# The end of a two-block decode attention: load order of the last pairs, V as the stationary operand in PV of five pairs, and wo as the stationary operand in the second block's output

## The chip, the cores and the metric

The kernel runs on one core of one Trainium2 chip. Its time is the device time of that core in microseconds (us), the median of several executions. A profile is one execution; the "span" that it shows is from the first to the last instruction and is about 1.8 us shorter than the time of the same execution. Times inside a profile count from the span's start. TensorE is PE (weight loads are PEld), VectorE is DVE, ScalarE is ACT, SyncE is SP.

## The reference, cut to what matters

Two independent attention blocks, A and B, each for one token, 32 heads, 8192 keys of 128 elements in bf16. The outputs stand side by side.

```
q      = x @ wq                                   # (512) @ (512 x 4096)
scores = einsum("bhqd,bhkd->bhqk", q, k_cache) * 128**-0.5
p      = softmax(scores)
o      = einsum("bhqk,bhkd->bhqd", p, v_cache)
y      = o.reshape(1, 1, 4096) @ wo               # (4096) @ (4096 x 512)
```

Each head's K is 2 MB and so is its V, and every byte is used once: 285 MB are read and almost nothing is written.

## The kernel before

Heads are handled in pairs: pairs 0 to 15 are block A, 16 to 31 block B. Below, "K30" is the 4 MB of keys of pair 30, "V30" its values. All loads go through a ring of five slots of 4 MB, in one fixed order on one queue; a slot is loaded anew when the last reader of its old content is done.

```
order = [('wq', a) for a in range(NA)]
for j in range(NPR + 1):                 # NPR = 32 pairs
    if j < NPR:      order.append(('k', j))
    if j == NPR - 1: order[-1:] = [('wo', LA), order[-1]]     # wo of B ahead of K31
    if j >= 1:       order.append(('v', j - 1))
    if j == PPA + 2: order.append(('wo', 0))
# so it ends: K30, V29, wo of B (first 24 heads), K31, rest of wo, V30, V31 in four parts
```

For one pair, VectorE multiplies K with q in place, in eight pieces (`plan_M`, about 1.17 us each); TensorE adds up the 128 products of each key with 2 x 16 matmuls against the identity (`plan_fold`; 3.6 us for one half at full clock); VectorE finishes the sums (`plan_R`), then come the maximum (`plan_m1`, a transpose `plan_tr`, `plan_m2`), exp on ScalarE, and PV on TensorE. PV has two forms. The wide one has p as the stationary operand, and its result must be copied out and turned:

```
def wide(e):                                   # pairs 0 to 29, plan_PV
    for i in range(0, TP, TB):                 # 32 matmuls, 512 columns each
        m = e.matmul(ot_ps[j % 2][0:2 * TB, :], p2[...i:i + TB...], t[:, i:i + TB, :]..., ...)
cp_val[j] = INC('ACT', c_cp, lambda e: e.copy(o8[:, j % 2, :], ot_ps[j % 2][0:2 * TB, :]))
...                                            # plan_ot: four f32 matmuls that turn o8

def op(e):                                     # pairs 30 and 31, plan_PVs
    for i in range(t0, t1):                    # up to 128 weight loads, 2 columns each
        m = e.matmul(ot_ps[j % 2][:, 0:2], t[:, i, :], p2[:, j % 2, i, :], ...)
```

y is o times wo. For all but the last four heads of B wo is loaded in a layout that makes its DMA pieces long, so o must be rearranged to fit it: `plan_w` does this for a block of n heads with n small matmuls on TensorE and some small operations on VectorE. y itself has a spread column of o as the stationary operand (4 columns wide, `sq`), with four matmuls of 128 columns for a head:

```
m = e.matmul(y_ps[0:NB, 0:P], sq[:, a, h0 + i, b * NB:(b + 1) * NB], wo[:, h0 + i, b, :], ...)
```

All engines work through fixed lists in order. TensorE's list ended: ..., PV29, max of pair 30 and 31 with y of B's heads 0 to 23 between, folds of K31, half of PV30, the block of heads 24 to 27, the rest of PV30, PV31 by parts, y of the last four heads.

## Time and profile before

| what | before | where it is read |
|---|---|---|
| time, median of the first 3 runs | 682.48 us (680.91 to 684.72) | timed runs |
| span | 680.3 us | page |
| DMA rate in midstream | about 431 GB/s | slice table |
| landing of V30; of V31's four parts | 659.3; 664.2, 666.6, 667.9, 669.1 | issue time plus time to landing |
| issue of the output's DMA | 678.42 us | timeline |

The lines below are from the page of before: the DMA's busy tenths, and the GB/s, in 40 equal slices.

```profile
span 680.3 us, 6183 instructions
...
DMA  9999999999999999999999999999999999999991
GB/s 370 432 432 431 432 431 432 433 430 432 431 432 429 432 434 433 432 431 432 431 430 431 432 433 431 432 431 432 431 429 433 432 432 431 432 431 420 421 423 63
```

The reader should see that there is no hole in the stream until the last slice. The Trainium skill, "DMA: Bandwidth & Descriptors", section "Where 436 GB/s comes from", gives 435 GB/s as the ceiling of the fabric; the 431 of this trace lie just below it, though above the 358 GB/s per core that the same section says binds loads from HBM, so here the measurement decides. The bytes can't shrink, so what can be saved is behind the stream.

The next view gives the same core in stretches of one microsecond (stretch, its length, busy time of PE, PEld, DVE, ACT, POOL with counts of instructions, granted clock, share of the DMA engines that were busy, GB/s).

```profile
662.00:663.00 1.00, 1.00 (x8) 0.39 (x3) 0.00 (x0) 0.49 (x3) 0.00 (x0) 1.00 0.98 406
...
664.00:665.00 1.00, 1.00 (x7) 0.00 (x0) 0.00 (x0) 0.00 (x0) 0.00 (x0) 1.00 0.63 258
...
667.00:668.00 1.00, 0.94 (x34) 0.84 (x31) 0.53 (x3) 0.00 (x0) 0.00 (x0) 1.00 0.19 78
668.00:669.00 1.00, 0.28 (x6) 0.31 (x6) 0.68 (x4) 0.00 (x0) 0.00 (x0) 1.00 0.10 41
```

The 16 engines do not finish together: the share falls from 0.98 to 0.10 within six microseconds. A load counts as landed when the last of its parts has: the packed trace marks 16 of them for each load. The 29.4 MB from K29's landing (599.5) to the last (669.1) came at 422 GB/s, and the prediction calls this the slowest engine's rate.

The third view is the chain of waits in order of time (start, length, what), here its tail.

```profile
615.75 31.09 DMA ring<-in_B_k_cache_dram
...
650.87 4.84 PE yps L615 x64
...
660.25 1.88 PE yps L615 x32
...
666.12 1.60 PE otps L514 x64
...
670.08 1.77 PE otps L514 x64
...
674.93 1.81 PE otps L514 x64
...
678.12 0.28 DVE y_sb L626
```

The last wait for data is K31's, which lands at 646.8. From there on everything is TensorE's and VectorE's own work: y of the first 24 heads (L615), PV30 and PV31 (L514). V31's first part, there at 664.2, is multiplied after 672. TensorE is late, not the data.

### The profile page before, as it was taken

Reading aid. Unit: us, or ns where it says so; the run is one execution under the profiler, and the core shown is the slowest. Engines: PE = TensorE matmul, PEld = TensorE weight load, DVE = VectorE, ACT = ScalarE, POOL = GpSimd, SP = SyncE. Lnnn points to the kernel's source line nnn. Section 1 sums busy time; section 2 is a strip of 40 time slices with the busy share of each in tenths; the row PEclk is TensorE's granted clock in tenths of the full one; section 3 lists DMA queues with packets and bytes.
Section 4 is the critical chain, followed back from the end, with each engine's and each line's share of the span. In section 5 each row is a group of like instructions: output and inputs, shape, how many; then the busy total and the mean of one; then the engine's idle time right before and its main releaser. Section 6 shows DMA issues by size and latency. Waiting matters only on the chain.

```text
span 680.3 us, 6183 instructions
## 1 busy us (share of the span) xinstructions
PE 561.4 (83%) x3020; PEld 168.8 (25%) x2060; DVE 386.4 (57%) x519; ACT 59.7 (9%) x199; POOL 2.4 (0%) x16
## 2 busy tenths in 40 slices
PE   0477998788799878887998496999789969876978
PEld 0120222122222212222221133232122212222246
DVE  4148656666555566665545626676655376663361
ACT  0020111101110111011101010111011101100000
POOL 1000000000000000000000000000000000000000
PEclk9998999889998988899988797999899979989887
DMA  9999999999999999999999999999999999999991
GB/s 370 432 432 431 432 431 432 433 430 432 431 432 429 432 434 433 432 431 432 431 430 431 432 433 431 432 431 432 431 429 433 432 432 431 432 431 420 421 423 63
DMA packets 11387, 285.61 MB, mean 420 GB/s; under 512 B 1504, under 2 KB 2016, under 8 KB 2400
## 3 DMA queue, kind: packets, MB, share of 16 engines
q1 hardware_dynamic: 11064, 285.22, 97.7%
q8 instruction: 20, 0.33, 0.2%
q10 hardware_dynamic: 296, 0.00, 0.0%
q14 instruction: 7, 0.06, 0.0%
HBM read 285.21 MB, written 0.00 MB: 419 GB/s over the span
## 4 chain that ended last, share of the span: by engine, by line
PE 44%; DMA 43%; DVE 11%; ACT 1%; issue 1%; ACTq 0%; DVEq 0%
DMA ring<-in_B_k_cache_dram 20%; DMA ring<-in_A_k_cache_dram 20%; PE fold L175 18%; PE otps L492 14%; DVE ring L387 8%; DMA xT<-in_B_x_dram 3%; PE qwps L359 3%; PE yps L615 2%; PE stps L532 2%; PE fold L171 2%; DVE s_sb L413 1%; PE otps L514 1%; DVE m L423 1%; ACT qbc L366 1%; PE stps L442 1%
## 5 line engine op out<-in xcount | busy, mean ns | idle before, releaser
L387 DVE TENSOR_TENSOR ring<-ring,qbc 128x2048 bf16<-128x2048 bf16 x256 | 298.3, 1215 | 154.1 <-DMA ring<-in_A_k_cache_dram 89.9
L175 PE MATMUL fold<-ring,ident 128*128 128x512 bf16 x960 | 245.9, 414 | 0.0
L492 PE MATMUL otps<-ring,p 128*8 128x512 bf16 x960 | 212.1, 379 | 0.0
L492 PEld LDWEIGHTS otps<-ring,p 128*8 128x8 bf16 x960 | 81.0, 87 | 116.4
L171 PE MATMUL fold<-ring,ident 128*128 128x512 bf16 x64 | 26.8, 419 | 53.3 <-DVE ring L387 53.3
L532 PEld LDWEIGHTS stps<-ident_f,o 8*128 8x128 f32 x240 | 28.9, 186 | 132.4 <-issue 132.4
L413 DVE TENSOR_REDUCE s_sb<-fold 128x64 f32<-128x512 f32 x64 | 44.0, 687 | 12.9 <-PE fold L175 12.5
L359 PE MATMUL qwps<-ring,xsel 128*128 128x512 bf16 x64 | 18.6, 442 | 29.1 <-DVE xsel L243 24.2
L502 ACT COPY o<-otps 8x512 f32<-8x512 f32 x30 | 17.3, 575 | 284.3 <-PE otps L492 284.3
L463 PEld LDWEIGHTS stps<-rowsum,ones_f 128*128 128x128 f32 x64 | 12.3, 194 | 98.7 <-issue 97.9
L432 PE MATMUL stps<-ident_f,m 128*2 128x128 f32 x32 | 9.2, 286 | 32.4 <-DVE m L423 32.3
L532 PE MATMUL stps<-ident_f,o 8*128 8x2 f32 x240 | 31.5, 249 | 0.0
L448 ACT COPY nb<-stps 128x1 f32<-128x1 f32 x32 | 5.1, 159 | 283.2 <-PE stps L442 283.2
L456 ACT ACTIVATE p<-s_sb,nb 64x128 bf16<-64x128 f32 x64 | 28.0, 437 | 1.9
L551 DVE TENSOR_TENSOR ot<-stps,rinv 128x2 bf16<-128x2 f32 x30 | 4.8, 159 | 40.3 <-PE stps L532 40.0
L171 PEld LDWEIGHTS fold<-ring,ident 128*128 128x128 bf16 x64 | 6.2, 97 | 62.3 <-DVE ring L387 58.2
L579 DVE TENSOR_TENSOR wt<-qwps,hmask 128x512 f32<-128x512 f32 (+3 forms) x5 | 2.2, 441 | 32.0 <-PE qwps L572 31.9
L423 DVE TENSOR_REDUCE m<-s_sb 64x1 f32<-64x128 f32 x64 | 17.9, 280 | 2.1
L615 PE MATMUL yps<-ring,sq 128*4 128x128 bf16 x256 | 17.3, 233 | 1.1 <-DVE sq L593 0.8
L615 PEld LDWEIGHTS yps<-ring,sq 128*4 128x4 bf16 x256 | 16.0, 91 | 1.8 <-issue 1.1
L359 PEld LDWEIGHTS qwps<-ring,xsel 128*128 128x128 bf16 x64 | 6.3, 108 | 40.8 <-issue 28.7
L432 PEld LDWEIGHTS stps<-ident_f,m 128*2 128x2 f32 x32 | 2.6, 80 | 48.6 <-DVE m L423 46.0
(37 smaller groups left out, 98.0 us busy)
## 6 DMA issues: line engine op xcount, KB each, us to landing
ring<-in_A_k_cache_dram SPq DMA_DIRECT2D x16, 4096.0 KB, 34.9
ring<-in_A_v_cache_dram SPq DMA_DIRECT2D x16, 4096.0 KB, 32.4
ring<-in_B_k_cache_dram SPq DMA_DIRECT2D x16, 4096.0 KB, 34.0
ring<-in_B_v_cache_dram SPq DMA_DIRECT2D x15, 4096.0 KB, 32.7
ring<-in_A_wq_dram SPq DMA_DIRECT2D x1, 4096.0 KB, 12.4
ring<-in_B_wq_dram SPq DMA_DIRECT2D x1, 4096.0 KB, 21.8
ring<-in_A_wo_dram SPq DMA_DIRECT2D x1, 4096.0 KB, 36.2
ring<-in_B_wo_dram SPq DMA_DIRECT2D x1, 2048.0 KB, 30.8
```

The costliest lines, as they stand in the source:

```text
L171: return e.matmul(out, lhsT, rhs, start=start, stop=stop)
L175: return e.add_instruction(mybir.InstMatmult(name=nc.get_next_instruction_name(), engine=e.engine, ins=[e.lower_ap(rhs), e.lower_ap(lhsT)] ...
L359: m = e.matmul(qw_ps[:, :].rearrange("p (j d) -> p j d", d=Dh), xsel[:, a, c, par, :], wq[:, c, 4 * g:4 * g + 4, par, :], start=(i == 0), ...
L387: m_val[(j, i)] = INC('DVE', c_m, lambda e: e.tensor_tensor(t, t, qbc[:, a, jj:jj + 1, :].broadcast_to([P, CH, Dh]), ALU.mult))
L413: r_val[(j, h)] = INC('DVE', c_r, lambda e: e.tensor_reduce(s_sb[:, j % 2, h * HT:(h + 1) * HT], fold_ps[h][:, :].rearrange("p (t e) -> p ...
L423: m1_val[j] = INC('DVE', c_m1, lambda e, h=h, q0=q0, q1=q1: e.tensor_reduce(m1[q0:q1, j % 2, h:h + 1], s_sb[q0:q1, j % 2, :], AX.X, ALU.max))
L456: e_val[j] = INC('ACT', c_e, lambda e, h=h, q0=q0, q1=q1: e.activation(p2[q0:q1, j % 2, :, h], s_sb[q0:q1, j % 2, :], AF.Exp, bias=nb[q0:q ...
L463: s_val[j] = INC('PE', c_s, lambda e: e.matmul(st_ps[j % 2][:, P + 2:P + 4], ones_f[:], rowsum[:, j % 2, :], start=True, stop=True))
L492: m = e.matmul(ot_ps[j % 2][0:2 * TB, :], p2[:, j % 2, i:i + TB, :].rearrange("p t h -> p (t h)"), t[:, i:i + TB, :].rearrange("p t d -> p ...
L502: cp_val[j] = INC('ACT', c_cp, lambda e: e.copy(o8[:, j % 2, :], ot_ps[j % 2][0:2 * TB, :]))
L532: m = e.matmul(st_ps[j % 2][:, OC:OC + 2], o8[:, j % 2, i * Dh:(i + 1) * Dh], ident_f[0:2 * TB, 2 * i:2 * i + 2], start=(i == 0), stop=(i ...
L615: m = e.matmul(y_ps[0:NB, 0:P], sq[:, a, h0 + i, b * NB:(b + 1) * NB], wo[:, h0 + i, b, :], start=(first and i == 0 and b == 0), stop=(las ...
```

## The change

Its intent is to have nothing left to do for the pair that lands last but a short PV. K30 and K31 land before V29, so the long path from K to p is done by the time V30 lands; the last load of all is wo of the last two heads, which is needed only after PV31. PV of the last five pairs has V stationary: 128 short matmuls and no copy and no turning. y of B's other 28 heads has wo stationary, with one column of o moving; it is gathered as a column in `y_bulk` and joined to the last heads by one f32 matmul. Block A's y becomes 32 matmuls of 512 columns.

```diff
+    NWIDE = NPR - 5                                  # was NPR - 2
...
-        for j in range(NPR + 1): ...                 # wo of B ahead of K31
+        for j in range(NPR):
+            order.append(('k', j))
+            if j >= 1:
+                order.append(('v', j - 1))
+            ...
+        order[-4:] = [order[-4], order[-2], ('wo', LA), order[-3], order[-1], ('v', NPR - 1)]
...
-        wo_early = wo_plan[LA][:sum(b[2] for b in wo_plan[LA]) - 1]
+        wo_early = wo_plan[LA][:-1]                  # the last block follows V31
...
+            def turned(e):
+                for i in range(t0, t1):
+                    m = e.matmul(ot_ps[j % 2][:, 0:2], t[:, i, :], p2[:, j % 2, i, :], ...)
+            OP('PE', wide if j < NWIDE else turned)
...
+            def cols(e):                             # y of B, heads 0 to 27
+                for i in range(n):
+                    for b in range(NB):
+                        m = e.matmul(y_ps[:, b:b + 1], wo_of(a)[:, h0 + i, b * P:(b + 1) * P],
+                                     w_bf[:, a, h0 + i:h0 + i + 1], ...)
...
+        # the tail of the program, after K31's folds
+        for b in early[:1]: plan_y(LA, *b[:2])       # heads 0 to 15
+        plan_tr(j); plan_m2(j)
+        for b in early[1:]: plan_y(LA, *b[:2])       # heads 16 to 23
+        plan_bc(j); plan_PV(j - 2); plan_exp(j); plan_o(j - 2); plan_sum(j); plan_ri(j)
+        plan_w_ready(j - 2)                          # heads 24 to 27
+        for b in perm_l[len(early):]: plan_y(LA, *b[:2])
+        plan_PV(j - 1); plan_o(j - 1); plan_ysq(0)
+        for i, (t0, t1) in enumerate(LAST_PARTS):
+            W('PE', *part_of[i]); plan_PV(j, t0, t1)
+        plan_o(j); plan_ysq(1)
```

More of the change, by code (lines that the diff above doesn't have):

```diff
@@ L125, in bass_concat_heads__mha_block_cached__gqa_block_cached__decode_kernel @@
         w_bf = ec(nc.sbuf_tensor("w_bf", [P, NA, H], BF16))
-        y_sb = ec(nc.sbuf_tensor("y_sb", [NB, NA, P], BF16))
-        sq = ec(nc.sbuf_tensor("sq", [P, NA, H, NB * NB], BF16))
+        y_row = ec(nc.sbuf_tensor("y_row", [1, NOUT], BF16))
+        y_bulk = ec(nc.sbuf_tensor("y_bulk", [P, NB], F32))
+        y_sb = ec(nc.sbuf_tensor("y_sb", [NB, P], BF16))
+        sq = ec(nc.sbuf_tensor("sq", [P, NDIR, NB * NB], BF16))
         fold_ps = [ec(nc.psum_tensor("fold%d" % i, [P, 512], F32)) for i in range(2)]
@@ L260, in bass_concat_heads__mha_block_cached__gqa_block_cached__decode_kernel @@
         order = [('wq', a) for a in range(NA)]
-        for j in range(NPR + 1):
-            if j < NPR:
-                order.append(('k', j))
-            if j == NPR - 1:
-                order[-1:] = [('wo', LA), order[-1]]
+        for j in range(NPR):
+            order.append(('k', j))
             if j >= 1:
                 order.append(('v', j - 1))
-            if j == PPA + 2:
+            if j == min(PPA + 2, NPR - 3):
                 order.append(('wo', 0))
+        order[-4:] = [order[-4], order[-2], ('wo', LA), order[-3], order[-1], ('v', NPR - 1)]
+        assert order[-6:-2] == [('k', NPR - 2), ('k', NPR - 1), ('wo', LA), ('v', NPR - 3)]
         assert order[-1] == ('v', NPR - 1)
@@ L305, in issue @@
             else:
-                early = wo_early if idx == LA else wo_plan[idx]
-                for blk in early:
-                    v = load_wo(idx, s, blk, s_part[4] if idx == LA else s_slot[s])
-                    land_of[('wo', idx, 0)] = (s_part[4] if idx == LA else s_slot[s], v)
-            if (kind, idx) == ('k', NPR - 1):
-                for blk in wo_plan[LA][len(wo_early):]:
-                    v = load_wo(LA, slot_of[('wo', LA)], blk, s_part[5])
-                    land_of[('wo', LA, 1)] = (s_part[5], v)
+                for blk in wo_early if idx == LA else wo_plan[idx]:
+                    land_of[('wo', idx, 0)] = (s_slot[s], load_wo(idx, s, blk, s_slot[s]))
+            if (kind, idx) == ('v', NPR - 1):
+                land_of[('wo', LA, 1)] = (s_part[5], load_wo(
+                    LA, slot_of[('wo', LA)], wo_plan[LA][-1], s_part[5]))
         def load_wo(a, s, blk, ctr):
@@ L430, in plan_tr @@
                 W('PE', c_ri, ri_val[j - 2])
-                W('PE', c_o, o_val[j - 2])
+                if j - 2 < NWIDE:
+                    W('PE', c_o, o_val[j - 2])
             tr_val[j] = INC('PE', c_tr, lambda e: e.transpose(
@@ L468, in plan_ri @@
             W('DVE', c_s, s_val[j])
+            if j >= 2:
+                W('DVE', c_o, o_val[j - 2])
             ri_val[j] = INC('DVE', c_ri, lambda e: e.reciprocal(
@@ L477, in bass_concat_heads__mha_block_cached__gqa_block_cached__decode_kernel, with plan_PV @@
         TB = 512 // Dh
-        NWIDE = NPR - 2
         cp_val, ot_val = {}, {}
-        def plan_PV(j):
-            assert j < NWIDE
-            landed('PE', ('v', j))
+        def plan_PV(j, t0=0, t1=TP):
+            if ('v', j) in land_of:
+                landed('PE', ('v', j))
             W('PE', c_e, e_val[j])
-            if j >= 2:
-                W('PE', c_cp, cp_val[j - 2])
+            if t0 == 0 and j >= 2:
+                if j - 2 < NWIDE:
+                    W('PE', c_cp, cp_val[j - 2])
+                else:
+                    W('PE', c_o, o_val[j - 2])
             t = kv(('v', j))
-            v = pv_val[j] = c_pv.bump()
             def wide(e):
-                for i in range(0, TP, TB):
+                for i in range(t0, t1, TB):
                     m = e.matmul(ot_ps[j % 2][0:2 * TB, :],
@@ L495, in wide @@
                                  start=(i == 0), stop=(i == TP - TB))
-                m.then_inc(c_pv.sem, 1)
-            OP('PE', wide)
-            release(('v', j), (c_pv, v))
-            W('ACT', c_pv, v)
-            if j >= 2:
-                W('ACT', c_ot, ot_val[j - 2])
-            cp_val[j] = INC('ACT', c_cp, lambda e: e.copy(
-                o8[:, j % 2, :], ot_ps[j % 2][0:2 * TB, :]))
-        def plan_PVs(j, t0, t1):
-            t = kv(('v', j))
-            W('PE', c_e, e_val[j])
-            if t0 == 0:
-                W('PE', c_cp, cp_val[j - 2])
-            def op(e):
+                if t1 == TP:
+                    m.then_inc(c_pv.sem, 1)
+            def turned(e):
                 for i in range(t0, t1):
@@ L517, in op @@
                     m.then_inc(c_pv.sem, 1)
-            OP('PE', op)
-            if t1 == TP:
-                pv_val[j] = c_pv.bump()
-                release(('v', j), (c_pv, pv_val[j]))
+            OP('PE', wide if j < NWIDE else turned)
+            if t1 < TP:
+                return
+            v = pv_val[j] = c_pv.bump()
+            release(('v', j), (c_pv, v))
+            if j < NWIDE:
+                W('ACT', c_pv, v)
+                if j >= 2:
+                    W('ACT', c_ot, ot_val[j - 2])
+                cp_val[j] = INC('ACT', c_cp, lambda e: e.copy(
+                    o8[:, j % 2, :], ot_ps[j % 2][0:2 * TB, :]))
         OC = P + 8
         def plan_ot(j):
+            if j >= NWIDE:
+                return
             W('PE', c_cp, cp_val[j])
@@ L543, in plan_o @@
                 src = st_ps[j % 2][:, OC:OC + 2]
-                dst = ot[:, a, 2 * jj:2 * jj + 2]
-                rin = rinv[:, j % 2, :]
             else:
                 W('DVE', c_pv, pv_val[j])
-                src = ot_ps[j % 2][:, 0:2, None].broadcast_to([P, 2, NB])
-                dst = sq[:, a, 2 * jj:2 * jj + 2, 0:NB * NB:NB + 1]
-                rin = rinv[:, j % 2, :, None].broadcast_to([P, 2, NB])
+                src = ot_ps[j % 2][:, 0:2]
+            dst = ot[:, a, 2 * jj:2 * jj + 2]
+            rin = rinv[:, j % 2, :]
+            if j >= NPR - NDIR // 2:
+                i = 2 * (j - NPR) + NDIR
+                src = src[:, :, None].broadcast_to([P, 2, NB])
+                dst = sq[:, i:i + 2, 0:NB * NB:NB + 1]
+                rin = rin[:, :, None].broadcast_to([P, 2, NB])
             o_val[j] = INC('DVE', c_o, lambda e: e.tensor_tensor(dst, src, rin, ALU.mult))
@@ L590, in red @@
                             wt[:, 0:ni * n].rearrange("p (i h) -> p i h", h=n), AX.X, ALU.add)
-                rv = INC('DVE', c_w, red)
-                W('DVE', c_w, rv)
-                w_val[(a, h0)] = INC('DVE', c_w, lambda e, i0=i0: e.tensor_copy(
-                    sq[:, a, h0 + i0:h0 + i0 + ni, 0:NB * NB:NB + 1],
-                    w_bf[:, a, h0 + i0:h0 + i0 + ni, None].broadcast_to([P, ni, NB])))
-        def plan_y(a, h0, n, pm):
-            W('PE', *land_of[('wo', a, int(a == LA and (h0, n, pm) not in wo_early))])
-            if pm:
-                W('PE', c_w, w_val[(a, h0)])
-            else:
-                W('PE', c_o, o_val[a * PPA + (h0 + n) // 2 - 1])
-            first = a not in y_started
-            y_started.add(a)
+                w_val[(a, h0)] = INC('DVE', c_w, red)
@@ L605, in plan_y, with wo_of, row @@
+        def wo_of(a):
+            return ring[:, slot_of[('wo', a)], 0:H * NOUT].rearrange("p (h n) -> p h n", h=H)
+        def plan_y(a, h0, n):
+            W('PE', *land_of[('wo', a, 0)])
+            W('PE', c_w, w_val[(a, h0)])
+            first = h0 == 0
             if first and a:
                 W('PE', c_ye, a)
-            lastblk = (h0 + n == H)
-            v = c_y.bump() if lastblk else None
-            def op(e):
-                wo = ring[:, slot_of[('wo', a)], 0:H * NOUT].rearrange(
-                    "p (h b m) -> p h b m", h=H, b=NB)
+            last = not any(pm and b > h0 for b, _, pm in wo_plan[a])
+            v = c_y.bump() if last else None
+            def row(e):
+                for i in range(n):
+                    m = e.matmul(y_ps[0:1, :], w_bf[:, a, h0 + i:h0 + i + 1], wo_of(a)[:, h0 + i, :],
+                                 start=(first and i == 0), stop=(last and i == n - 1),
+                                 skip_group_check=True)
+                if last:
+                    m.then_inc(c_y.sem, 1)
+            def cols(e):
@@ L613, in op @@
                 for i in range(n):
                     for b in range(NB):
-                        m = e.matmul(y_ps[0:NB, 0:P], sq[:, a, h0 + i, b * NB:(b + 1) * NB],
-                                     wo[:, h0 + i, b, :],
+                        m = e.matmul(y_ps[:, b:b + 1], wo_of(a)[:, h0 + i, b * P:(b + 1) * P],
+                                     w_bf[:, a, h0 + i:h0 + i + 1],
                                      start=(first and i == 0 and b == 0),
-                                     stop=(lastblk and i == n - 1 and b == NB - 1),
+                                     stop=(last and i == n - 1), skip_group_check=True)
@@ new lines, in cols @@
+                if last:
+                    m.then_inc(c_y.sem, 1)
+            OP('PE', cols if a == LA else row)
+            if not last:
+                return
+            W('ACT', c_y, v)
+            if a != LA:
+                release(('wo', a), (c_y, v))
+                ve = INC('ACT', c_ye, lambda e: e.copy(y_row[:], y_ps[0:1, :]))
+                W('ACT', c_ye, ve)
+                s_out.bump(16)
+                OP('ACT', lambda e: e.dma_start(
+                    out[0, 0:1, a * NOUT:(a + 1) * NOUT], y_row[:]).then_inc(s_out.sem, 16))
+                return
@@ new lines, in plan_y, with plan_ysq, op @@
+            ve = INC('ACT', c_ye, lambda e: e.copy(y_bulk[:], y_ps[:, 0:NB]))
+            W('PE', c_ye, ve)
+            if qw_free[0]:
+                W('PE', *qw_free[0])
+            OP('PE', lambda e: e.matmul(qw_ps[0:NB, 0:P], y_bulk[:], ident_f[:],
+                                        start=True, stop=False, skip_group_check=True))
+        def plan_ysq(i):
+            h0, n, _ = direct_l[i]
+            last = i == len(direct_l) - 1
+            W('PE', *land_of[('wo', LA, int(last))])
+            W('PE', c_o, o_val[LA * PPA + (h0 + n) // 2 - 1])
+            v = c_y.bump() if last else None
+            def op(e):
+                for k in range(n):
+                    for b in range(NB):
+                        m = e.matmul(qw_ps[0:NB, 0:P], sq[:, 2 * i + k, b * NB:(b + 1) * NB],
+                                     wo_of(LA)[:, h0 + k, b * P:(b + 1) * P],
+                                     start=False, stop=(last and k == n - 1 and b == NB - 1),
@@ L619, in op @@
                                      skip_group_check=True)
-                if lastblk:
+                if last:
                     m.then_inc(c_y.sem, 1)
             OP('PE', op)
-            if lastblk:
-                release(('wo', a), (c_y, v))
+            if last:
+                release(('wo', LA), (c_y, v))
                 W('DVE', c_y, v)
-                ve = INC('DVE', c_ye, lambda e: e.tensor_copy(y_sb[:, a, :], y_ps[0:NB, 0:P]))
-                q = 'SP' if a == LA else 'ACT'
-                W(q, c_ye, ve)
+                ve = INC('DVE', c_ye, lambda e: e.tensor_copy(y_sb[:], qw_ps[0:NB, 0:P]))
+                W('SP', c_ye, ve)
@@ L629, in plan_y @@
                 s_out.bump(16)
-                OP(q, lambda e: e.dma_start(
-                    out[0, 0, a * NOUT:(a + 1) * NOUT].rearrange("(b m) -> b m", b=NB),
-                    y_sb[:, a, :]).then_inc(s_out.sem, 16))
+                OP('SP', lambda e: e.dma_start(
+                    out[0, 0, LA * NOUT:(LA + 1) * NOUT].rearrange("(b m) -> b m", b=NB),
+                    y_sb[:]).then_inc(s_out.sem, 16))
         for a in range(NA):
@@ L662, in bass_concat_heads__mha_block_cached__gqa_block_cached__decode_kernel @@
                 plan_tr(j - 1)
-            if j == NPR - 1:
-                for b in wo_early[:1]:
-                    plan_y(LA, *b)
             plan_fold(j, 0)
-            if j >= 2:
+            if 2 <= j < NPR - 1:
                 plan_ot(j - 2)
-            if j == NPR - 1:
-                for b in wo_early[1:]:
-                    plan_y(LA, *b)
             plan_M(j, 4)
@@ L679, in bass_concat_heads__mha_block_cached__gqa_block_cached__decode_kernel @@
             plan_M(j, 7)
-            if j >= 2:
+            if 2 <= j < NPR - 1:
                 plan_o(j - 2)
@@ L685, in bass_concat_heads__mha_block_cached__gqa_block_cached__decode_kernel @@
                 plan_sum(j - 1)
-            if j < NPR - 1:
-                if c:
-                    plan_PV(j - 1)
-                if j == PPA + 1:
-                    for h0, n, pm in wo_plan[0]:
-                        plan_w(0, h0, n)
-                if j == PPA + 2:
-                    for h0, n, pm in wo_plan[0]:
-                        plan_y(0, h0, n, pm)
+            if c and j < NPR - 2:
+                plan_PV(j - 1)
+            if j == PPA + 1:
+                for h0, n, pm in wo_plan[0]:
+                    plan_w(0, h0, n)
+            if j == PPA + 2:
+                for h0, n, pm in wo_plan[0]:
+                    plan_y(0, h0, n)
+            if j < NPR - 1:
                 plan_w_ready(j - 2)
@@ L700, in bass_concat_heads__mha_block_cached__gqa_block_cached__decode_kernel @@
         plan_m1(j)
-        landed('PE', ('v', j - 1))
-        plan_PVs(j - 1, 0, HT)
+        early = [b for b in perm_l if b[0] in w_done]
+        for b in early[:1]:
+            plan_y(LA, *b[:2])
         plan_tr(j)
-        plan_w_ready(j - 2)
-        assert len(w_done) == len(perm_l)
-        plan_m2(j)
-        for b in perm_l[len(wo_early):]:
-            plan_y(LA, *b)
-        plan_bc(j)
-        plan_exp(j)
-        plan_PVs(j - 1, HT, TP)
-        plan_sum(j)
+        plan_m2(j)
+        for b in early[1:]:
+            plan_y(LA, *b[:2])
+        plan_bc(j)
+        plan_PV(j - 2)
+        plan_exp(j)
+        plan_o(j - 2)
+        plan_sum(j)
+        plan_ri(j)
+        plan_w_ready(j - 2)
+        assert len(w_done) == len(perm_l) and len(direct_l) == 2
+        for b in perm_l[len(early):]:
+            plan_y(LA, *b[:2])
+        plan_PV(j - 1)
         plan_o(j - 1)
-        plan_ri(j)
-        assert len(direct_l) == 2
+        plan_ysq(0)
         for i, (t0, t1) in enumerate(LAST_PARTS):
             W('PE', *part_of[i])
-            plan_PVs(j, t0, t1)
-            if i == 0:
-                plan_y(LA, *direct_l[0])
+            plan_PV(j, t0, t1)
         plan_o(j)
-        plan_y(LA, *direct_l[1])
+        plan_ysq(1)
         assert issued[0] == len(queue)
```

## The prediction

> **What bounds the kernel now.** The load stream. In the slice table the DMA engines are at 9 tenths in 39 of 40 slices, at about 431 GB/s; the Trainium skill ("DMA: Bandwidth & Descriptors", section "Where 436 GB/s comes from") puts the ceiling at 435; the trace agrees, and the stream can't get shorter: the bytes are the same. Only what follows it can be saved. From the issues' times to landing, V30 lands at 622.9+36.4 = 659.3 us, the parts of V31 at 664.2, 666.6, 667.9 and 669.2. The span is 680.3: 11.1 us come after the last byte, 1.9 of them (from 678.4) the output's DMA.
>
> In the tail TensorE is late, not the data. K31 lands only at 646.86 (VectorE waits 9.97 us for it), and its multiply, folds, max and exp come ahead of PV30 and PV31. In the timeline PE is busy without a gap from 650.5 to 667.8: y of the first heads 4.91 + 1.95 us, two folds of 3.6, PV30's first half only at 665.98. V31's first part, landed at 664.2, is multiplied at 672.1, the rest at 674.87 to 676.7; then o, 8 matmuls of y (1.01), a copy (0.28).
>
> **What changes.** (1) K31 moves ahead of wo and V29. With the slowest engine's rate of 422 GB/s (29.4 MB from K29's landing, 599.56, to 669.2) I estimate landings: K30 619.5, K31 629.4, wo but its last two heads 638.7, V29 648.7, V30 658.6, V31's parts 663.6, 666.1, 667.3, 668.6, the last wo 669.2. (2) PV of the last five pairs: 128 matmuls with V stationary instead of 32 wide ones: 7.07 us becomes 3.6 (64 such took 1.74 to 1.86 us, 28 ns each; the skill, "TensorE: Matmul & The Clock Gate", section "Back-to-back issue gap", gives a floor of about 25 ns, and the trace agrees). The ACT copy (0.57) and the transposes (1.05) go. (3) y of B with wo stationary: 96 matmuls, 6.86 us, become about 2.7; a copy on ACT and one f32 matmul are added, about 1 us, before V30 lands. A's y becomes 32 wide matmuls, off the path.
>
> **On the critical path.** K31's fold should end near 648, PV29 run at 651 to 655, y's bulk end at 658, PV30 at 658.6 to 662.2, y of pair 30 at 663.3. Then PE waits for V31's parts and has 0.5 us left after the last: 669.1. o 0.2, y 1.0 (after the last wo, 669.2), copy 0.3: 670.7, plus 1.95 for the output: span 672.6, 7.7 us less. Midstream PE time is slack and saves nothing.
>
> **Prediction.** 682.5 - 7.7, about 674.5 us; 8 in 10: 671.5 to 677.5. Faster by over 2% (under 668.8): 4%; within 2%: 95%; slower: 1%.
>
> **What would show it.** The last landing within 1 us of 669; K31 near 629; in the chain of waits the last long piece is DMA into the ring, not PE; PE idle before V30 and V31's parts; PV groups of 128 at 28 ns each; y's 64 matmuls near 1.8 us; from the last landing to the output's issue about 1.5 us instead of 9.2.
>
> **What would make it wrong.** A cold PE clock, or VectorE's two back-to-back K pairs, making PE late at V30 by more than the 2 to 3 us of slack; wo's 1 KB pieces at the very end landing late (their delay counts in full); the stream stalling where a slot is released late; wo-stationary matmuls slower than 28 ns.

## The result, and the profile after

The change has 675.06 us (674.81 to 676.53, four runs) against 683.03 of before (680.91 to 684.72, four runs). The ratio is 0.9889, 95% interval 0.9857 to 0.9921. Ratios here and below are the mean time of one kernel's fast runs over that of the other's of the same rounds, so not quite the ratio of the medians quoted. It is 1.1% faster: within 2%, as forecast, and 0.6 us from the forecast time.

The page of the change, in the same lines as before:

```profile
span 673.0 us, 6543 instructions
...
DMA  9999999999999999999999999999999999999995
GB/s 374 436 436 429 425 427 428 435 436 432 430 425 432 430 435 432 430 429 428 433 429 433 432 429 429 429 436 430 431 429 429 432 427 436 429 427 431 421 427 238
```

And its chain of waits, the tail, in order of time:

```profile
583.77 35.31 DMA ring<-in_B_k_cache_dram
...
619.10 2.36 DVE ring L387 x2
...
625.95 4.97 PE fold L178 x15
...
639.18 4.92 PE fold L178 x15
...
648.09 1.60 PE yps L621 x64
...
650.93 1.36 PE otps L506 x51
652.29 1.37 issue
653.66 2.23 PE otps L506 x77
...
659.65 3.52 PE otps L506 x128
...
664.50 0.57 PE otps L506 x18
665.07 1.13 issue
666.21 3.11 PE otps L506 x110
...
669.73 1.03 PE qwps L657 x8
...
670.78 0.28 DVE y_sb L667
```

Three readings. First, the stream ends where it did: issue times plus times to landing give K31 at 629.8, V30 at 658.6, V31's parts at 663.5, 666.0, 667.2 and 668.5, and the last wo at 669.2 (before: last landing 669.1). From there to the output's issue it was 9.3 us (669.1 to 678.42), it is 1.9 (669.16 to 671.09): this difference of 7.4 us is the gain in span, 7.3. Secondly, the chain does not end in the stream: its last DMA is K30, landed at 619.08, and from there it is VectorE and TensorE throughout. PV30 starts at 659.65, 1.0 us after V30 has landed, and no part of V31 is waited for. Two chains, the stream and the path from K30, end within half a microsecond of each other in this execution. Thirdly, there are two gaps in the middle of PV (L506: after 51 matmuls of PV29 and after 18 of PV31) that the profile calls "issue": TensorE waited for nothing that is shown.

The number was right; which chain carries the end was not, so the number was in part luck. The experiments had to settle three things: which parts of the change bring the gain, which chain sets the end, and what the gaps are.

### The profile page after: what moved, and what is told of

Same layout as the page of the kernel before. It is cut to its first block, busy times and chain, and to the rows that moved or that the text cites. A ratio compares the mean times of both kernels' runs of the same rounds, so it can differ in the third digit from the quotient of the medians.

```text
span 673.0 us, 6543 instructions
## 1 busy us (share of the span) xinstructions
PE 546.7 (81%) x3190; PEld 159.2 (24%) x2230; DVE 384.8 (57%) x513; ACT 58.7 (9%) x198; POOL 2.4 (0%) x16
## 4 chain that ended last, share of the span: by engine, by line
DMA 45%; PE 42%; DVE 10%; issue 2%; ACT 1%; ACTq 0%; DVEq 0%
DMA ring<-in_B_k_cache_dram 21%; DMA ring<-in_A_k_cache_dram 20%; PE fold L178 18%; PE otps L497 14%; DVE ring L387 7%; DMA xT<-in_B_x_dram 3%; PE qwps L359 3%; PE fold L174 2%; PE stps L533 2%; PE otps L506 2%; DVE s_sb L413 1%; PE yps L612 1%; ACT qbc L366 1%; DVE m L423 1%; PE stps L443 1%
## 5 line engine op out<-in xcount | busy, mean ns | idle before, releaser
L178 PE MATMUL fold<-ring,ident 128*128 128x512 bf16 x960 | 248.6, 418 | 0.0
L497 PE MATMUL otps<-ring,p 128*8 128x512 bf16 x864 | 190.9, 379 | 0.0
L497 PEld LDWEIGHTS otps<-ring,p 128*8 128x8 bf16 x864 | 72.9, 87 | 104.8
L533 PEld LDWEIGHTS stps<-ident_f,o 8*128 8x128 f32 x216 | 26.0, 186 | 119.6 <-issue 119.6
L519 ACT COPY o<-otps 8x512 f32<-8x512 f32 x27 | 15.5, 574 | 255.7 <-PE otps L497 255.7
L533 PE MATMUL stps<-ident_f,o 8*128 8x2 f32 x216 | 28.3, 249 | 0.0
L506 PE MATMUL otps<-p,ring 128*128 128x2 bf16 x640 | 17.6, 164 | 2.5 <-issue 2.5
L506 PEld LDWEIGHTS otps<-p,ring 128*128 128x128 bf16 x640 | 17.3, 100 | 3.3 <-issue 3.3
L443 PEld LDWEIGHTS stps<-m,sel 2*128 2x128 f32 x64 | 9.5, 185 | 20.6 <-issue 20.6
```

The source lines that it names most:

```text
L178: return e.add_instruction(mybir.InstMatmult(name=nc.get_next_instruction_name(), engine=e.engine, ins=[e.lower_ap(rhs), e.lower_ap(lhsT)] ...
L443: bc_val[j] = INC('PE', c_bc, lambda e: e.matmul(st_ps[j % 2][:, P:P + 1], sel2[:], m2[0:2, j % 2:j % 2 + 1], start=True, stop=True))
L497: m = e.matmul(ot_ps[j % 2][0:2 * TB, :], p2[:, j % 2, i:i + TB, :].rearrange("p t h -> p (t h)"), t[:, i:i + TB, :].rearrange("p t d -> p ...
L533: m = e.matmul(st_ps[j % 2][:, OC:OC + 2], o8[:, j % 2, i * Dh:(i + 1) * Dh], ident_f[0:2 * TB, 2 * i:2 * i + 2], start=(i == 0), stop=(i ...
```

## The experiments

Twelve kernels ran; every one gave a correct result. The first four and the next four each ran on one chip with their own runs of before.

### 1 to 4: one part undone, or the order alone

`undo_order`: the changed kernel with the old load order and the old places of PV29 and y in the program.

```diff
-        order[-4:] = [order[-4], order[-2], ('wo', LA), order[-3], order[-1], ('v', NPR - 1)]
+        if j == NPR - 1: order[-1:] = [('wo', LA), order[-1]]      # as before
...
-            if c and j < NPR - 2:  plan_PV(j - 1)
+            if c and j < NPR - 1:  plan_PV(j - 1)
```

> The changed kernel with the old order of loads and the old places of PV29 and of y's first blocks in the program; PV of five pairs and y of B stay as changed. Theory (after the change the end of the stream, last landing 669.2 us, and the chain on TensorE end together, and the order alone lets K31's chain run before the stream ends): K31 lands near 646.9 again, the multiply, two folds (one at a cold clock, 5.6 us) and PV30, PV31 follow; I estimate a span near 678, so 2 us below before and 5 above the change. Rival (cheaper PV and y alone bring the gain, the order is decoration): span within 1 us of 673.0.

Measured: 680.23 us against 681.17, ratio 0.9973 (0.9958 to 0.9988), span 678.5. K31 landed at 646.9 again. As expected: cheaper PV and y alone are worth little, 1.8 us by the ratio (0.9 by the medians), because they still stand behind K31.

`undo_pv`: the changed kernel with `NWIDE = NPR - 2`, and the turning of pair 29 placed after the sum of pair 31.

> The changed kernel with the wide PV for pairs 27, 28 and 29 again (only the last two with V stationary). Theory: only PV29 counts, because it alone stands between V29's landing (648.9) and V30's (658.6): 7.07 us wide plus copy 0.57 and transposes 1.05 instead of 3.6 (and 1.37 of stall) makes TensorE start PV30 near 663 instead of 659.65; span near 675.5, 2.5 above the change. Rival (the 3.5 us saved per pair count for each of the three pairs): 10 us lost, span above 680.

Measured: 683.90 us, ratio 1.0029 (1.0009 to 1.0049), span 681.5, 8.5 more than the change. The theory fell: PV27 and PV28 count as well. The profile shows how. With PV28 wide, VectorE comes to the rearranging of o for B's heads 16 to 23, whose 8 matmuls stand behind PV28 in TensorE's list, and waits for them; the multiply of K30, next in VectorE's list, starts at 623.93 though K30 has landed at 619.2. In the change it started at 619.10. Experiments 8 to 12 follow this up; by the span of `three_turned` there (676.3), 3.3 of the 8.5 us belong to PV27 and PV28.

`undo_y`: y of B's 28 heads as before.

```diff
-  m = e.matmul(y_ps[:, b:b + 1], wo_of(a)[:, h0 + i, b * P:(b + 1) * P], w_bf[:, a, h0 + i:h0 + i + 1], ...)
+  m = e.matmul(y_ps[0:NB, 0:P], sqb[:, h0 + i, b * NB:(b + 1) * NB], wo_of(a)[:, h0 + i, b * P:(b + 1) * P], ...)
```

> The changed kernel with y of B's first 28 heads computed as before (the column of w stationary, four columns at a time, 112 matmuls at about 77 ns) into the bank that the last heads use too; the order and PV as changed. Theory: the 96 matmuls ahead of PV29 take 6.9 us instead of 2.7, TensorE is 3 to 4 us late at V30, span near 675.5. Rival (the first 24 heads' y hides behind the wait for V29): span unchanged within 0.5 us.

Measured: 677.46 us, ratio 0.9937 (0.9921 to 0.9954), span 675.5; the change has 0.9889 to 0.9904. The 96 matmuls of y took 3.73 + 1.95 us instead of 1.74 + 0.94, PV29 began at 655.1 (650.9) and PV30 at 662.85 (659.65). About 1.0 of these 4.2 us is not y's: K30 landed at 620.28 here instead of 619.08, and K31's second fold began at 645.34 instead of 644.35. The rival, that this y hides behind the wait for V29, fell: V29 had landed at 649.1.

`order_only`: both undone, so the new order alone.

> The new order of loads alone: wide PV for all but the last two pairs, y of B as before. Theory (parts do not add: what TensorE does between K31's folds and V31's landing must fit into about 10 us per load): TensorE is late by the sum of both, near 8 us, PV31 starts near 672 and the span is near 679, so the order alone saves only 1 to 2 us of 7.3. Rival (order is all of the gain): within 1 us of 673.

Measured: 686.44 us, ratio 1.0067 (1.0052 to 1.0082), span 684.4. The order alone makes the kernel 5 us slower than before, not 1 to 2 faster as I expected. The loads that it brings forward are of no use as long as TensorE and VectorE can't be done with them: the rearranging of heads 16 to 23 comes to VectorE only at 623.60, as in `undo_pv`, and then wide PV29 (now behind K31's folds) and the old y stand in front of V30. The last landing was 669.3, as ever; the output was issued at 682.48, 13 us later.

| kernel | order | PV of 5 pairs | y with wo stationary | ratio to before |
|---|---|---|---|---|
| `order_only` | new | no | no | 1.0067 |
| `undo_pv` | new | no | yes | 1.0029 |
| `undo_order` | old | yes | yes | 0.9973 |
| `undo_y` | new | yes | no | 0.9937 |
| the change (three sets of runs) | new | yes | yes | 0.9889, 0.9904, 0.9902 |

The parts do not add. The order makes 7 us available; PV and y make TensorE quick enough to take them.

### 5 to 8: the gaps, and TensorE's share in the middle

`again` is the change once more.

> The changed kernel once more, as the mate of the other runs of this call. Both theories: span 673.0 within 1 us; if the two gaps in PV (1.37 us after 51 matmuls of PV29, 1.13 us after 18 of PV31) are fetches of the instruction stream they stand at the same two matmuls again; if they are chance (clock, memory) they move.

`pad52` has 52 tiny matmuls more, each with its weight load, where TensorE waits for its first data:

```diff
+        for _ in range(52):
+            e.matmul(qw_ps[:, 0:2], ident[:], ident[:, 0:2], start=True, stop=True)
```

> The changed kernel with 52 tiny extra matmuls (104 instructions) on TensorE in the first microseconds, where it waits for data. Theory (in the trace, one 16 KB packet of the instruction queue comes per about 256 TensorE instructions; a group of 128 load-and-multiply pairs uses 256 in 3.6 us, faster than such a packet comes): the block borders move 104 instructions earlier in the stream, so the gap leaves the middle of PV29 (to its start or end) and that of PV31; TensorE starts PV30 at its landing (658.6) instead of 659.65, y's last block starts at wo's landing, and the end comes 0.3 to 0.5 us earlier. Rival (clock or data): the gaps stay where they are and the end moves by nothing.

`again`: 675.66 us (675.15 to 677.15), ratio 0.9904 (0.9885 to 0.9923). The gaps stood after the same 51 and 18 matmuls, 1.29 and 0.59 us long. `pad52`: 676.49 us, ratio 0.9914 (0.9895 to 0.9933). The timeline of TensorE in `pad52` (start, length, engine, line, operation, tiles, shapes, count, and the idle time before with what ended it):

```profile
651.00 3.38 PE L506 MATMUL otps<-p,ring 128*128 128x2 bf16 x127
655.96 0.16 PE L506 MATMUL otps<-p,ring 128*128 128x2 bf16 x1 [1.58 <-issue]
...
659.83 2.88 PE L506 MATMUL otps<-p,ring 128*128 128x2 bf16 x102
663.40 0.83 PE L506 MATMUL otps<-p,ring 128*128 128x2 bf16 x26 [0.68 <-issue]
...
665.51 2.66 PE L506 MATMUL otps<-p,ring 128*128 128x2 bf16 x94
669.32 1.05 PE L506 MATMUL otps<-p,ring 128*128 128x2 bf16 x34 [1.15 <-issue]
```

Counted in matmuls with their weight loads, a block of 256 instructions is 128 long. Shifted by 52, the gap after 51 of PV29 should come one matmul ahead of PV29 and again after 127: it is after 127. The one after 18 of PV31 should come 52 earlier, across the 8 matmuls of y, that is after 128 - (52 - 18 - 8) = 102 of PV30, and again at 94 of PV31 (102 + 128 - 8 - 128 = 94): it is at 102 and at 94. So the gaps belong to places in the instruction stream, with a period of 256: counted in the packed traces, exactly 256 TensorE instructions lie from one of these gaps to the next in `pad52`, and 512 in the change, in `again` and in `again2`. (The border between their two gaps falls after 26 matmuls of PV30 and shows none; its packet, from 657.61 to 658.69 in the change, had come before PV30 began.)

The trace has a DMA queue of instructions beside it, with 16 KB packets that come one for each 256 or so instructions of TensorE, 21 in the change and 20 before; in the change one ran from 651.27 to 652.29 and the next but one from 663.68 to 664.76, each ending some 1.4 us ahead of a gap's end (653.66 and 666.21). The kept traces of all runs have 17 such TensorE gaps over 0.25 us, and every one ends 1.2 to 1.5 us after such a packet does. The Trainium skill, "Runtime: NRT & Kernel Launch", section "Instruction fetch mechanics", says that instructions are refilled in blocks of 16 KiB or 256 instructions, which agrees, and that the cost is mostly hidden, which holds for 19 of the change's 21 packets (no gap over 0.25 us follows them) but not in PV29 and PV31: 128 weight loads and 128 matmuls are one block in 3.6 us, and the gaps were 0.4 to 2.1 us over all runs. The wide PV uses 64 instructions in 7.1 us, and before had no such gap over 0.25 us.

The forecast gain of 0.3 to 0.5 us did not come: the borders moved, but onto places just as bad (three gaps, 3.4 us in all, instead of 2.5 in the first profile of the change and 1.9 in that of its mate), and `pad52` was if anything slower than its mate. That the gaps are TensorE's wait for its next block of instructions is shown by their places and by the packets; that shifting them pays is not.

`all_turned` sets `NWIDE = 0`, V stationary in all 32 pairs.

> The changed kernel with V stationary in all 32 pairs. Theory (the stream bounds the middle, TensorE time there is slack): TensorE's work falls by some 27 x 4.5 = 120 us, but the time stays within 1% of the change; some 18 more 16 KB instruction packets at 1.07 us each ride on the same 16 DMA engines, so the last landing is 0 to 2 us later. Rival (TensorE, 81% busy, bounds the kernel): tens of us faster.

Measured: 681.65 us (680.31 to 682.04), ratio 0.9983 (0.9964 to 1.0002): 6 us slower than the change, though TensorE is busy for 460 us instead of 547. That TensorE bounds the middle is refuted. But the time did not stay either, and the page says why in part; the lines are the granted clock in 40 slices (tenths) and the instruction queue (packets, MB, share of the DMA engines):

```profile
PEclk9997776767877766778876587666788876777785
...
q8 instruction: 40, 0.66, 0.4%
```

The same lines of the change:

```profile
PEclk9998999889988979999888879989988979978785
...
q8 instruction: 21, 0.34, 0.2%
```

The mean granted clock is 0.762 instead of 0.917. In part TensorE is simply less busy (68% of the span instead of 81%). But matmuls of two columns did not bring the clock back even where TensorE was busy without a break. In before these microseconds are PV30, PV31 and a little y (same columns as the stretches above):

```profile
670.00:675.00 5.00, 5.00 (x144) 4.76 (x144) 0.35 (x2) 1.14 (x5) 0.00 (x0) 0.54 0.01 3
```

The clock fell to 0.50 at 670.4 and stayed there; folds in the change, by contrast, ran at 0.50 from 640 to 643 and at 1.00 from then on. Folds that follow a turned PV run slow: the mean of one of their matmuls (L178) is 457 ns instead of 418.

There are 19 more instruction packets of about 1.07 us; over 16 engines that is 1.3 us, my estimate. The last landing was 3.5 us later than in the change (672.7). Evenly spread, the packets explain 1.3 of these; the packed trace shows that they are not felt evenly. The first of the last load's 16 parts lands at 664.14 (664.10 in the change), the last 8.55 us later (5.06): the whole delay is in the parts that land last. For the 4 MB loads this spread grew from 0.84 us in five steps of 1.3 to 1.4 us, at the first landing after the 1st, 9th, 17th, 25th and 33rd packet (64.0, 183.3, 319.7, 448.7, 585.0 us), and by no more than 0.21 us at a time otherwise. So it seems that every eighth packet falls where it delays the landings; this is read from one trace, and no run tests it. The rest, to 5.7 us between the last landing and the output's issue (1.9 in the change), is TensorE's path at the low clock, with two gaps of 1.87 and 1.14 us in its PV and one of 1.13 us ahead of K30's multiply.

`three_turned` sets `NWIDE = NPR - 3`.

> The changed kernel with V stationary in the last three pairs instead of five. Theory (only PV29, PV30 and PV31 lie behind the last landings): same within 0.5 us, or better by a moved block border. Rival (PV27 and PV28 must be cheap too, for K30's fold): 3 to 7 us slower.

Measured: 679.38 us (677.76 to 680.98), ratio 0.9957 (0.9935 to 0.9978), 3.7 us over `again` beside it. The rival was right. VectorE's timeline of this run:

```profile
623.15 0.22 DVE L583 TENSOR_TENSOR wt<-qwps,hmask 128x64 f32<-128x64 f32 x1 [10.32 <-PE qwps L576]
...
623.54 2.35 DVE L387 TENSOR_TENSOR ring<-ring,qbc 128x2048 bf16<-128x2048 bf16 x2
```

VectorE sat idle for 10.32 us, ended by the 8 small matmuls behind PV28; K30, multiplied in the second line, had been there since 619.14. PV27 alone was not tested.

### 9 to 12: where the path from K30 loses its time

`again2` is the change a third time.

> The changed kernel a third time, as the mate of the two other runs of this call: 675.0 to 676.0 us median, ratio to before 0.989 to 0.991.

Measured: 675.96 us (674.61 to 677.07), ratio 0.9902 (0.9881 to 0.9924).

`three_w_late` is `three_turned` with the rearranging of heads 16 to 23 one pair later.

```diff
-            if j < NPR - 1:
+            if j < NPR - 1 and j != NPR - 3:
                 plan_w_ready(j - 2)
```

> The kernel with V stationary in the last three pairs (it had 679.4 us, 3.7 over the change), with one thing more: the rearranging of the outputs of B's heads 16 to 23 (8 small matmuls on TensorE behind PV28, two small operations on VectorE) is planned one pair later, behind K30's multiply. Theory (wide PV28 costs time only because VectorE, which works in order, waits for those 8 matmuls and so starts K30's multiply at 623.5 instead of at K30's landing, 619.1): multiply of K30 starts at 619.1, and 3 to 4 us come back, median near 676. Rival (TensorE's own time in PV27 and PV28, 7.1 us instead of 3.6 each, is what counts): stays near 679.

Measured: 677.99 us (677.58 to 678.10), ratio 0.9933 (0.9908 to 0.9958). VectorE's timeline:

```profile
619.04 2.36 DVE L387 TENSOR_TENSOR ring<-ring,qbc 128x2048 bf16<-128x2048 bf16 x2 [6.06 <-DMA ring<-in_B_k_cache_dram]
...
635.71 0.23 DVE L583 TENSOR_TENSOR wt<-qwps,hmask 128x64 f32<-128x64 f32 x1 [3.23 <-PE qwps L576]
...
636.10 2.35 DVE L387 TENSOR_TENSOR ring<-ring,qbc 128x2048 bf16<-128x2048 bf16 x2
```

K30's multiply now starts as K30 lands, as the theory said. But it is not clear that any time came back: the interval overlaps that of `three_turned` (0.9935 to 0.9978, on another chip), and the profiled runs of the two have spans of 676.4 and 676.3. I had moved the same wait ahead of K31's multiply, where VectorE again waits 3.23 us for the same matmuls, this time behind K30's folds, and starts at 636.10. K31 had landed at 629.7. The wait was moved, not removed. Three pairs with the wait removed were not run, so the rival, that TensorE's own 7.1 us for a wide PV28 is a part of the 3.7, is not excluded.

`w_late_y_early` makes the same move in the change itself, and puts y of heads 0 to 23 ahead of K31's first fold.

> The changed kernel (five pairs) with that rearranging one pair later, and with y of B's heads 0 to 23 ahead of K31's first fold, where TensorE waits for VectorE, with a landing semaphore of their own for their part of wo. Theory (after the change the end is set by TensorE's chain from K30 on, 0.4 to 2.7 us behind the stream, whose last landing is 669.2): PV29 starts 1.5 to 2 us earlier, PV30 at V30's landing (658.6), the span comes to 672.6 to 673.2 in every run, so a median near 674.5 and a smaller spread than the 675.2 to 677.2 of the change. Rival (the stream alone sets the end already): no difference from the change beside it.

Measured: 677.08 us (676.07 to 677.69), ratio 0.9918 (0.9895 to 0.9941), so 1.1 us slower by the medians than `again2` beside it (the two intervals overlap), against both the theory and the rival. The same mistake shows in VectorE's timeline:

```profile
636.06 0.22 DVE L585 TENSOR_TENSOR wt<-qwps,hmask 128x64 f32<-128x64 f32 x1 [3.49 <-PE qwps L578]
...
636.45 2.35 DVE L389 TENSOR_TENSOR ring<-ring,qbc 128x2048 bf16<-128x2048 bf16 x2
```

VectorE is idle for 3.49 us, ended by the same matmuls, so K31's multiply starts at 636.45 (632.16 in `again2`) and PV29 at 655.56 (651.67). Holding up this path made the end later while the last landing stayed at 669.1: the path from K30, and not the stream, carries the end here.

`w_at_last` mends this: the rearranging stands where VectorE comes to it only after TensorE is done with its part.

```diff
             if c:
                 plan_tr(j - 1)
+            if j == NPR - 1:
+                plan_w_ready(j - 3)              # heads 16 to 23
+                plan_y(LA, *perm_l[0][:2])       # heads 0 to 15, ahead of K31's first fold
             plan_fold(j, 0)
...
-            if j < NPR - 1:
+            if j < NPR - 1 and j - 2 < NPR - 5:
                 plan_w_ready(j - 2)
```

(The wo blocks of heads 0 to 23 have a landing semaphore of their own, as in the run before.)

> The changed kernel with the rearranging of heads 16 to 23 planned at the last pair, its 8 matmuls right behind that pair's first transpose (so they are done before VectorE, after the fourth multiply, comes to its two operations), and with y of heads 0 to 15 behind them, ahead of K31's first fold. The run before this one moved the same operations only one pair on, and VectorE then waited for the 8 matmuls ahead of K31's multiply (3.5 us) instead. Theory (the end is set by the chain VectorE-TensorE from K30 on): K30's multiply starts at its landing (619.1), K31's near 631.6, no wait of VectorE for those matmuls; PV29 starts near 649.5 instead of 650.9 to 653.9, PV30 at V30's landing 658.6 or within 0.5 us of it; span 672.6 to 673.5, median 674.2 to 675.0, so 0.987 to 0.988 of before, in every run under 676. Rival (the stream alone sets the end, or the lateness arises elsewhere): 0.989 to 0.991 of before as the change, spread as before.

Measured: 674.54 us, all six runs between 674.46 and 674.88; ratio 0.9891 (0.987 to 0.9911), span 672.7. TensorE's timeline of its end:

```profile
658.60 3.57 PE L508 MATMUL otps<-p,ring 128*128 128x2 bf16 x128 [0.76 <-DMA ring<-in_B_v_cache_dram]
...
664.89 2.89 PE L508 MATMUL otps<-p,ring 128*128 128x2 bf16 x95 [0.71 <-issue]
668.45 0.59 PE L508 MATMUL otps<-p,ring 128*128 128x2 bf16 x16 [0.67 <-DMA ring<-in_B_v_cache_dram]
669.47 1.01 PE L659 MATMUL qwps<-ring,sq 128*4 128x128 bf16 x8 [0.43 <-DVE sq L557]
```

and its chain of waits:

```profile
635.42 32.99 DMA ring<-in_B_v_cache_dram
...
668.45 0.60 PE otps L508 x16
...
670.52 0.28 DVE y_sb L669
```

Now TensorE waits for V30 and for V31's last part, and the chain ends in the stream. One instruction gap is left, 0.71 us, and costs nothing, since TensorE waits for V31's last part behind it. Is this version better than the change? Its ratio misses my 0.987 to 0.988, and its interval overlaps those of the change, so by the ratios it is not shown to be faster. What does differ is the scatter: 15 runs of the change, in three sets, lie between 674.61 and 677.15 with a median of 675.66, and only two of them are below the slowest of these six. Before had the same median, 682.48, in this set and in the set of `again2`, though on another chip. I read this as the removal of a delay of 0 to 2.5 us that the change has in some runs: in `again` K29's first fold took longer (5.97 us for 15 matmuls, 4.65 in the first profile of the change), so the rearranging came at 620.13 and K30's multiply at 620.5 instead of 619.1 (K30 had landed at 619.40). In the profile of `w_at_last` this fold was slow too (5.67 us), and K30's multiply still began at 619.04, as K30 landed.

## Why the prediction was right, point by point

- "The stream can't get shorter", and the landings: right. All ten forecast landings, from K30 to the last wo, are within 0.5 us of the measured ones (K31 629.4 against 629.8, V30 658.6 against 658.6, the last wo 669.2 against 669.2).
- V stationary, 3.6 us for 128: right, 3.57 where no gap fell (the skill's floor of about 25 ns a matmul, as quoted, agrees with 28 ns, though here each matmul has a weight load with it).
- y with wo stationary, 2.7 us for 96 matmuls: right, 1.74 + 0.94 us.
- Span 672.6: measured 673.0 in the profiled run, 672.9 to 675.3 over the 15 runs of the change and 672.7 to 673.2 in the six runs of `w_at_last`; time 674.5 against 675.06.
- "In the chain of waits the last long piece is DMA into the ring, not PE; PE idle before V30 and V31's parts": wrong for the change. Its last DMA is K30; PV30 was 1.0 us late and V31's parts were not waited for. The step that failed is "2 to 3 us of slack" at V30. My own sum left only 0.6 (y's bulk done at 658, V30 there at 658.6), and PE was free at 659.65, in `again` at 662.50. In the profiled run K31's folds ended at 647.97 and PV29 began at 650.93, both as forecast; what the sum lacked is the gap of 1.37 us in PV29, for which I had nothing, and room for the joining of y's parts, which I had sized at 1 us and which took 0.83 (658.82 to 659.65). In `again` K31's folds ended at 650.92 as well: the first folds of K29, K30 and K31 ran at a low clock (15 matmuls took 5.97, 5.96 and 5.67 us, those of the second folds 3.40). This I had named as a risk but not put into the sum. Even in `w_at_last`, which has neither the gap in PV29 nor the wait of VectorE, the slack was 0.76 us. Two chains end almost together, and that is why the time came out right all the same: here it was luck.
- "Midstream PE time is slack and saves nothing": right for the middle (`all_turned`: 87 us less work, no gain), wrong for PV27 and PV28 together, which I took to be midstream. What the traces show is that VectorE waits, for the rearranging of o, behind PV28.
- From the last landing to the output's issue "about 1.5 us": 1.9 in the change, 1.76 in `w_at_last` (669.07 to 670.83).

## What to carry to other kernels

When a load stream is the bound, look at what is still undone when the last bytes land, order the loads so that the longest dependent path starts earliest, and then check that the compute engines can take what the new order offers: here the order alone cost 5 us and the whole change gained 7. An engine that works in order can be held up by a two-operation chore whose partner stands behind a long job on another engine; moving such a chore is safe only to a place where the partner is surely done. When a forecast time comes true, look at whether the forecast chain did, too.

## What the Trainium skill lacked or had wrong

- "Runtime: NRT & Kernel Launch", "Instruction fetch mechanics": it calls the crossing of a 16 KiB block mostly hidden. That holds for most blocks here, but in 128 weight loads with 128 two-column matmuls, one block in 3.6 us, with the DMA engines full of data, TensorE stood still for 0.4 to 2.1 us at a border (1.37 and 1.13 us in the change). It says that the fetches have a DMA queue of their own, but not what they cost a load stream that fills the engines; here 19 more packets came with a last landing 3.5 us later, and in that trace the landings were set back after every eighth packet, by 1.3 to 1.4 us.
- "TensorE: Matmul & The Clock Gate", "What's actually happening": it says that the clock follows how busy TensorE has been, but not that weight loads with two-column matmuls do not count for much. In before, from 670 to 675 us, TensorE is busy all the time with almost nothing else, and the granted clock is 0.54. In the stretch from 660 to 670 us of the change TensorE's matmuls are busy for 8.10 of 10 us and its weight loads for 7.66, and the granted clock is 0.50; with V stationary in all pairs the mean clock is 0.762 instead of 0.917.
- "DMA: Bandwidth & Descriptors": it gives the rate of all engines together (435 GB/s, 431 here). It has no figure for how far the 16 engines drift apart in a long stream: here the share of busy engines fell from 0.98 to 0.10 over six microseconds, the 16 parts of a load landed 0.5 us apart early in the stream and 5 us apart at its end, and the last 29.4 MB landed at 422 GB/s, which is the number that a forecast of the end needs.
